# Packed attention with an MLP behind it, on one core: the held PSUM pair in a pool of its own, and another order of the inserted blocks

## The chip, the core and the metric

The kernel runs on one core of one Trainium2 chip. The metric is the device time of one execution in microseconds (us). Three runs of the kernel before gave 245.87, 245.77 and 245.65, a median of 245.77. One more execution was taken with the hardware profiler; it is the one that the rows of this document come from, and it took 245.88, of which 244.1 is the span that the profile covers. Its granted TensorE clock was 0.998 of full speed.

## What is computed

```python
def sm_attn(qq, kk, vv):
    s = scale * np.matmul(qq, kk.transpose(0, 1, 3, 2))
    a = np.exp(s - np.max(s, axis=-1, keepdims=True))
    a = a / (np.sum(a, axis=-1, keepdims=True) + 1e-09)
    return np.matmul(a, vv)
p_packed = sm_attn(p, k, v)            # 32 packed queries per head
out = sm_attn(q, p_packed, p_packed)   # 576 queries against 32 keys
x = out.transpose(0, 2, 1, 3).reshape(4608, 512)
h = x @ w_in                           # 512 x 2048
return (h * cos(h)) @ w_out            # 2048 x 512
```

There are 8 batches, 8 heads, 576 positions and a head dimension of 64.

## The kernel before

Everything but the softmax sums is done in bf16 with sums in fp32. The kernel never forms the second attention's output: for each batch it multiplies the packed result with `w_in` first (`ppw`, four pieces of 512 columns, into `PPW`), and then the normalised second softmax `a2n` with `PPW`. That gives `h` transposed, in 16 blocks of 128 of the 2048 columns (a block is called fc, 0 to 15).

The order of the work is written out by hand; tiles get their semaphores from the framework, and each engine works through its own queue in the order in which the instructions were recorded. For a batch b the steps are:

- `pe_T` (transposes of k or q on TensorE, L121) or `xbar` (by a DMA, L107), `s1` (scores and exp of the first softmax), `a1_pe`/`a1_xbar`, `pp` (packed result, L191), `pp_T` (L203), `ppw` (L218), `s2` (scores and exp of the second softmax, L148), `sums2` (L244) and `normalise`, which gives `a2n`.
- 16 blocks. `h_mm` (L268) does four matmuls of 288 columns into a pair of PSUM banks, ScalarE takes the cosine (L272), VectorE the product into `gT` (L275). Batch 0 is different: `h_one` (L294) does two matmuls of 512 columns into one bank, cosine at L299, product at L300; its last 64 rows of all blocks follow later in `h_rest` (L308), whose product goes to `joint` (L314).
- The second product of the MLP, `gT` with `w_out`, in chunks of 128 rows and 16 matmuls each. These matmuls are called fills: a generator yields them one by one, and `fill(n)` puts the next n into TensorE's queue, wherever the hand-written order has room. `out_gen` (L359) serves batches 1 to 7, `out_first` (L375) batch 0.

PSUM has 8 banks. Pool `O` holds two for the whole kernel (`ot`). The other six change owner: `banks("pairs")` makes them three pairs, A0, A1 and A2 (pool `psA`), and `banks("single")` six single banks (pool `psH`); the old pool is closed first, so the new one's tiles wait for the readers of the old. `psa` hands the pairs out in turn, as `pairs` lists them. Batch 0's 16 blocks run in the single banks, taken in rotation; behind them come the first fills of batch 0 and `ppw(1, 0)` and `ppw(1, 1)`, also in single banks, and then the pairs are opened again.

`out_first` opens four chunks of batch 0 at once: chunks 0 and 1 in the two banks of `O`, chunks 2 and 3 in a held pair, A2 (`psa(at=2)`, so it needs the pairs). It yields 4 fills of each chunk, again 4 of each, then finishes chunks 2 and 3 in the slot of batch 1, frees A2 and finishes chunks 0 and 1. `store` copies a finished chunk to `osb` with one engine (`osb_eng`, ScalarE in a slot) and issues its DMAs on SP.

```python
    set_filler(0)
    fill(4)
    for n in range(2):
        ppw(1, n, (ACT, V), own=one)
    fill(4)
    ACT.preload_act_table_set(EXP_SET)
    banks("pairs")
    fill(4)
...
    fill(4)
    s2(1)
```

Between the last two `fill(4)` stand the 24 transposes of q of batch 1 and the copies to `qT` by VectorE and ScalarE.

Batch 1's 16 `h_mm` blocks are called its slot. `slot(1, hooks, trail, heavy, weight)` puts `weight[fc]` fills behind block fc (the weights sum to 36, as many as the fills left with the 8 of batch 1 that trail) and the hooks named for that fc; `heavy[fc] = (_, n)` keeps up to n of the block's fills behind the hook. A block without an entry in `heavy` has its fills behind the hook. The hooks are `pw2` (`ppw(1, 2)` and `ppw(1, 3)`, each a pair, the first half copied by ScalarE and the second by VectorE), `h_rest(0)`, two DMA transposes on SP (k of batch 3, q of batch 2), `pack_p` (transposes of p for batches 2 and 3) and the transposes of k of batch 2 (`tk2` and `pe_T`). Behind the slot come ScalarE's table load, four fills and `s1(2)`.

Of the kernel before, what the change touches and what calls it, by code (L numbers as in the profile page):

```python
# [8 lines left out]
FP32 = mybir.dt.float32  # L9
# [6 lines left out]
def kernel(  # L16
# [19 lines left out]
    PSUM = bass.MemoryType.PSUM  # L36
# [11 lines left out]
    o_pool = ctx.enter_context(tc.tile_pool(name="o", bufs=4))  # L48
    small = ctx.enter_context(tc.tile_pool(name="small", bufs=3))
    O = ctx.enter_context(tc.tile_pool(name="psO", bufs=2, space=PSUM))  # L50
    ctx.enter_context(tc.manual_schedule())
    psum = {"stack": ctx.enter_context(ExitStack())}

    pairs, turn = [], [0]

    def banks(kind):

        psum["stack"].close()
        name, n = ("psA", 1) if kind == "pairs" else ("psH", 6)
        psum[name] = psum["stack"].enter_context(tc.tile_pool(name=name, bufs=n, space=PSUM))  # L60
        pairs[:], turn[0] = [0, 1, 2], 0

    banks("pairs")
    V, ACT, G = nc.vector, nc.scalar, nc.gpsimd

# [18 lines left out]
    def copy(eng, out, in_):  # L84
        if eng is ACT:
            ACT.copy(out=out, in_=in_)  # L86
        else:
            eng.tensor_copy(out=out, in_=in_)  # L88

    def psa(dt=FP32, at=None):  # L90

        if at is None:
            at = pairs[turn[0] % len(pairs)]
            turn[0] += 1
        return psum["psA"].tile([128, 2, 512 if dt == FP32 else 1024], dt, name="psA", tag=f"A{at}")

    def load(n, b):
        bf[n, b] = bf_pool.tile([TP, H, C * D], BF16, name=n + "bf", tag=n + "bf", bufs=1 if n == "q" else 2)
# [13 lines left out]
    def pe_T(n, b, engs=(V, V, V), groups=(0, 1, 2), own=None):  # L112
        if 0 in groups:
            xT[n, b] = att_pool.tile([128, H * 3, TP], BF16, name=n + "T", tag=n + "T", bufs=2 if n == "k" else 1)
        t = xT[n, b]
        flat = bf[n, b].rearrange("p h x -> p (h x)")
        for i in groups:
            ps = own(BF16) if own else psa(BF16)[:, 0, :]
            for j in range(8):
                o = 8 * i + j  # L120
                nc.tensor.transpose(ps[:, j * TP:(j + 1) * TP], flat[:, o * 128:(o + 1) * 128],  # L121
                                    ident[0:TP, 0:TP])
            to = t[:, 8 * i:8 * i + 8].rearrange("p a x -> p (a x)"), ps[:, 0:8 * TP]
            if engs[i] is None:
                return to
            copy(engs[i], *to)

    def bank(dt=FP32):
        return O.tile([128, 512 if dt == FP32 else 1024], dt, name="ot", tag="ot")

    def pack_p(b0, b1, flat=None):
        ng = 2 * (b1 - b0)
        if flat is None:
            flat = psa(BF16).rearrange("p a x -> p (a x)")
        for g in range(ng):
            nc.tensor.transpose(flat[:, g * 128:(g + 1) * 128],
                                p_bf[:, 2 * b0 + g].rearrange("p t d -> p (t d)"), ident)
        V.tensor_copy(out=P2[:, b0:b1].rearrange("p b h n -> p (b h n)"), in_=flat[:, 0:ng * 128])
# [67 lines left out]
    def ppw(b, n, eng=None, own=None, later=False, cuts=((0, 512),)):  # L206
        if b not in PPW:
            PPW[b] = ppw_pool.tile([128, 2, DF], BF16, name="PPW", tag="PPW")
        two = isinstance(eng, tuple)
        if own:  # L210
            ps = [own(), own()]
        else:
            t = psa()
            ps = [t[:, 0, :], t[:, 1, :]]
        for x in range(4):
            for y in range(2):
                r = slice(64 * y, 64 * y + 64)
                nc.tensor.matmul(ps[y][32 * x:32 * x + 32, :], ppT[b % 2][r, 0, x, :],  # L218
                                 w_in_bf[r, x, n * 512:(n + 1) * 512], start=True, stop=True)

        def evacuate(cuts=cuts):
            if own or two:
                for a, z in cuts:
                    for y in range(2):
                        copy(eng[y] if two else eng, PPW[b][:, y, n * 512 + a:n * 512 + z], ps[y][:, a:z])
            else:
                copy(eng or (V, ACT)[n % 2], PPW[b][:, :, n * 512:(n + 1) * 512], t)
        if later:
            return [lambda c=c: evacuate((c,)) for c in cuts]
        evacuate()  # L230

    def s2(b):
        a2u[b] = att_pool.tile([128, 2, S], BF16, name="a2u", tag="a2u")
        ps = scores(lambda r, h, e: ppT[b % 2][r, (h + e) % 2, h // 2, :], xT["q", b])
        for y in range(2):
            ACT.activation(out=a2u[b][:, y].rearrange("p (e x) -> p e x", e=2),  # L236
                           in_=ps[y][:, :, 0:HS], func=AF.Exp, scale=rs1[b][:, y:y + 1])
# [80 lines left out]
    osb_eng = [V]  # L318

    def pieces_of(b, c):  # L320
        ob = out[b * S:(b + 1) * S, :].rearrange("(p c) d -> c p d", c=C)
        if c == 4:
            o0 = out[(b - 1) * S:b * S, :].rearrange("(p c) d -> c p d", c=C)
            return [(0, 64, o0[5, 32:96]), (64, 128, ob[5, 32:96])]
        res, z = [], c * 128
        while z < c * 128 + 128:
            j, p0 = z // TP, z % TP
            n = min(TP - p0, c * 128 + 128 - z)
            res.append((z - c * 128, z - c * 128 + n, ob[2 * (j % 3) + j // 3, p0:p0 + n]))
            z += n  # L330
        return res

    def n_chunks(b):
        return 5 if b % 2 and b < B - 1 else 4

    def tail_chunk(b, c):
        osb = o_pool.tile([128, DM], FP32, name="osb")
        for i, (a, z) in enumerate(((0, 256), (256, 384), (384, 512))):
            cols = slice(a, z)
            ps = O.tile([128, z - a], FP32, name="ot", tag="ot")  # L340
            for fc in range(NFC):
# [3 lines left out]
            for (a, z, rows), q in zip(pieces_of(b, c), (nc.sync, nc.scalar)):  # L345
                q.dma_start(out=rows[:, cols], in_=osb[a:z, cols])

    def store(b, c, ps):
        osb = o_pool.tile([128, DM], FP32, name="osb")
        copy(osb_eng[0], osb, ps)  # L350
        for a, z, rows in pieces_of(b, c):
            nc.sync.dma_start(out=rows, in_=osb[a:z, :])

    def out_gen(b):
        for c in range(n_chunks(b)):
            ps = O.tile([128, DM], FP32, name="ot", tag="ot")
            for fc in range(NFC):
# [6 lines left out]
    def out_first():  # L364

        pss = {}
        for c, fcs in ((0, 4), (1, 4), (2, 4), (3, 4), (0, 8), (1, 8), (2, 8), (3, 8),
                       (2, 12), (3, 12), (2, 16), (3, 16), (0, 16), (1, 16)):
            if c not in pss:
                if c == 2:  # L370
                    held = psa(at=2)
                    pairs[:] = [0, 1]
                pss[c] = O.tile([128, DM], FP32, name="ot", tag="ot") if c < 2 else held[:, c - 2, :]
            for fc in range(8 if (c, fcs) in ((0, 16), (1, 16)) else fcs - 4, fcs):
                nc.tensor.matmul(pss[c], gT[0][:, fc, c * 128:(c + 1) * 128], w_out_bf[:, fc, :],  # L375
                                 start=(fc == 0), stop=(fc == NFC - 1))
                if fc == NFC - 1 and c == 3:
                    store(0, 2, pss[2])
                    store(0, 3, pss[3])
                    pairs[:], turn[0] = [0, 1, 2], 0  # L380
                elif fc == NFC - 1 and c < 2:
                    store(0, c, pss[c])
                yield
# [3 lines left out]
    def set_filler(b):  # L387
        filler.append([out_gen(b) if b else out_first(), 16 * n_chunks(b)])
# [4 lines left out]
    def fill(n):  # L393
        while n > 0 and filler:
            next(filler[0][0])
            filler[0][1] -= 1
            if filler[0][1] == 0:
                filler.pop(0)
            n -= 1
# [9 lines left out]
    def dup_p(a, b, eng):  # L409
        for t in range(2):  # L410
            eng.tensor_copy(out=p_bf[:, a:b, t, :], in_=p_raw[:, a:b, :])
# [74 lines left out]
    c14()()  # L486
    c15()()
    set_filler(0)
    fill(4)
    for n in range(2):  # L490
        ppw(1, n, (ACT, V), own=one)
    fill(4)
    ACT.preload_act_table_set(EXP_SET)
    banks("pairs")
    fill(4)
    t = psa(BF16)
    for i in range(2):
        pe_T("q", 1, (None,) * 3, (i,), own=lambda dt: t[:, i, :])
# [3 lines left out]
    load("q", 2)  # L502
    load("v", 2)
    dup_p(4, 2 * B, G)
    fill(4)
    s2(1)
    fill(4)
    sums2(1, 0)
# [28 lines left out]
    def pw2(b, n, eng=None):  # L537
        ppw(b, n, eng)
        ppw(b, n + 1, eng)
# [20 lines left out]
    def cross(n, b):  # L560
        return lambda: xbar(n, b)

    osb_eng[0] = ACT
    slot(1, [(5, lambda: pw2(1, 2, (ACT, V))), (6, lambda: h_rest(0)), (7, cross("k", 3)),
             (8, lambda: pack_p(2, 4)), (9, cross("q", 2)), (10, tk2), (11, lambda: pe_T("k", 2, (V, V, ACT), (2,)))],
         trail=8, heavy={5: (0, 2), 6: (0, 2)}, weight=[3, 3, 3, 3, 2, 3, 3, 2, 2, 2, 2, 2, 2, 2, 1, 1])
    ACT.preload_act_table_set(EXP_SET)
    osb_eng[0] = V
    behind(xT["q", 2][0:1, 0, 0:1])
# [110 lines left out]
```

## Time and profile before

| | |
|---|---|
| median of three runs | 245.77 us |
| the profiled execution | 245.88 us, span 244.1 us |
| TensorE matmuls | 230.0 us busy, 2208 rows |
| VectorE | 161.3 us busy, 256 rows |
| ScalarE | 167.1 us busy, 267 rows |
| batch 0's blocks, first to last product | 23.36 to 34.73 us |
| `s2(1)`, first matmul | 38.84 us |
| batch 1's slot, first matmul | 44.15 us |
| `s1(2)`, first matmul | 65.26 us |

PE is TensorE, PEld its weight loads, DVE VectorE, ACT ScalarE, POOL GpSimd, SP the engine that issues most DMAs. A row of the timeline gives start, duration, engine, line, operation, output and input tiles, and how many instructions of the kind were joined (x4). In brackets stands how long the engine was idle before and what ended that. Consecutive matmuls overlap: a matmul of 512 columns has a row of 0.38 us, but the next one starts 0.22 later, so four of them have a joint row of 1.04. A few matmul records are missing from the trace.

### The profile page before, as it was taken

Reading aid. Unit: us, or ns where it says so; the run is one execution under the profiler, and the core shown is the slowest. Engines: PE = TensorE matmul, PEld = TensorE weight load, DVE = VectorE, ACT = ScalarE, POOL = GpSimd, SP = SyncE. Lnnn points to the kernel's source line nnn. Section 1 sums busy time; section 2 is a strip of 40 time slices with the busy share of each in tenths; the row PEclk is TensorE's granted clock in tenths of the full one; section 3 lists DMA queues with packets and bytes.
Section 4 is the critical chain, followed back from the end, with each engine's and each line's share of the span. In section 5 each row is a group of like instructions: output and inputs, shape, how many; then the busy total and the mean of one; then the engine's idle time right before and its main releaser. Section 6 shows DMA issues by size and latency. Waiting matters only on the chain.

```text
span 244.1 us, 5438 instructions
## 1 busy us (share of the span) xinstructions
PE 230.0 (94%) x2208; PEld 128.1 (52%) x2244; DVE 161.3 (66%) x256; ACT 167.1 (68%) x267; POOL 37.6 (15%) x60
## 2 busy tenths in 40 slices
PE   7889889999999999999999999999999999999994
PEld 3454335556555564565546564556456554565453
DVE  3359981668658986687757787678758688787001
ACT  2349996687839868876978677876788583776110
POOL 8522212201130014005100501030100110010000
PEclk9999999999999999999999999999999999999999
DMA  6999999999799999999999995989376101311133
GB/s 94 202 205 207 205 205 227 198 228 207 143 148 195 223 202 139 219 220 189 220 182 193 156 209 107 183 168 208 69 150 142 46 0 46 86 43 46 44 85 86
DMA packets 64376, 37.37 MB, mean 153 GB/s; under 512 B 36864, under 2 KB 59776, under 8 KB 64352
## 3 DMA queue, kind: packets, MB, share of 16 engines
q0 software_dynamic: 23152, 18.75, 50.5%
q1 hardware_dynamic: 40960, 18.16, 34.7%
q8 instruction: 17, 0.28, 0.4%
q10 hardware_dynamic: 240, 0.13, 0.2%
q14 instruction: 7, 0.06, 0.1%
HBM read 37.22 MB, written 9.44 MB: 191 GB/s over the span
## 4 chain that ended last, share of the span: by engine, by line
PE 79%; DVE 7%; ACT 2%; issue 2%; ACTq 0%
PE ot L359 43%; PE psA L268 22%; DVE gT L300 3%; PE psA L375 3%; PE psA L218 2%; PE psA L148 2%; PE ot L375 1%; PE ot L342 1%; PE psA L244 1%; DVE PPW L88 1%; DVE gT L275 1%; PE psA L191 1%; ACT cosT L272 1%; PE psA L121 1%; DVE joint L314 1%
## 5 line engine op out<-in xcount | busy, mean ns | idle before, releaser
L359 PE MATMUL ot<-w_out_bf,gT 128*128 128x512 bf16 x424 | 109.8, 379 | 2.1 <-issue 1.6
L275 DVE TENSOR_TENSOR gT<-psA,cosT 128x576 bf16<-128x576 f32 x112 | 83.2, 757 | 21.9 <-ACT cosT L272 20.9
L272 ACT ACTIVATE cosT<-psA 128x576 bf16<-128x576 f32 x112 | 72.8, 654 | 25.2 <-PE psA L268 24.0
L268 PE MATMUL psA<-a2n,PPW 128*128 128x288 bf16 x448 | 73.2, 286 | 0.4
L359 PEld LDWEIGHTS <-gT 128*128 128x128 bf16 x448 | 42.2, 98 | 37.4 <-issue 4.2
L268 PEld LDWEIGHTS <-PPW 128*128 128x128 bf16 x448 | 43.7, 98 | 30.2 <-issue 0.9
L88 DVE CAST PPW<-psA 128x1024 bf16<-128x1024 f32 (+1 forms) x21 | 24.3, 1170 | 7.9 <-PE psA L218 7.9
L279 POOL COPY joint<-gT 128x512 bf16<-128x512 bf16 x14 | 8.7, 618 | 91.5 <-DVE gT L275 91.5
L88 DVE COPY osb<-ot 128x512 f32<-128x512 f32 (+2 forms) x17 | 11.0, 647 | 15.6 <-PE ot L342 14.6
L86 ACT COPY osb<-ot 128x512 f32<-128x512 f32 (+1 forms) x19 | 10.8, 568 | 14.3 <-PE ot L359 9.1
L254 DVE SCALAR_TENSOR_TENSOR a2n<-a2u,r,lns 128x576 bf16<-128x576 bf16 x16 | 12.4, 814 | 12.3 <-ACT lns L252 12.3
L246 ACT ACTIVATE lns<-psA 128x576 f32<-128x576 f32 x16 | 10.4, 652 | 7.3 <-PE psA L244 6.8
L157 ACT ACTIVATE a<-psA 128x576 bf16<-128x576 f32 x16 | 10.3, 647 | 7.3 <-PE psA L148 7.2
L359 PE MATMUL ot<-w_out_bf,joint 128*128 128x512 bf16 x45 | 14.0, 379 | 0.3 <-issue 0.2
L236 ACT ACTIVATE a2u<-psA,rs 128x576 bf16<-128x576 f32 x16 | 11.0, 738 | 1.4 <-PE psA L148 1.4
L103 POOL COPY gate<-kT 1x1 bf16<-1x1 bf16 x4 | 0.7, 181 | 64.7 <-DMA kT<-kbf 64.7
L300 DVE TENSOR_TENSOR gT<-psH,cosT 128x512 bf16<-128x512 f32 x16 | 9.9, 685 | 0.4 <-ACT cosT L299 0.4
L252 ACT ACTIVATE lns<-lns 128x576 f32<-128x576 f32 x16 | 10.0, 676 | 0.0
L218 PE MATMUL psA<-w_in_bf,ppT 64*32 64x512 bf16 x208 | 9.2, 380 | 0.4 <-DVE gT L275 0.4
L299 ACT ACTIVATE cosT<-psH 128x512 bf16<-128x512 f32 x16 | 8.9, 633 | 0.7 <-DVE gT L300 0.4
L416 PE MATMUL ot<-wz 128*128 128x512 f32 (+2 forms) x11 | 7.5, 769 | 1.9 <-DVE wz L429 1.7
L375 PE MATMUL ot<-w_out_bf,gT 128*128 128x512 bf16 x30 | 8.8, 380 | 0.1
(89 smaller groups left out, 191.9 us busy)
## 6 DMA issues: line engine op xcount, KB each, us to landing
kbf<-in_k_dram POOLq DMA_DIRECT2D x8, 576.0 KB, 13.0
vbf<-in_v_dram POOLq DMA_DIRECT2D x8, 576.0 KB, 7.9
qbf<-in_q_dram POOLq DMA_DIRECT2D x8, 576.0 KB, 10.5
out_dram<-osb SPq DMA_DIRECT2D x24, 192.0 KB, 3.9
out_dram<-osb SPq DMA_DIRECT2D x22, 128.0 KB, 2.5
w_in_bf<-in_moe_w_in_dram POOLq DMA_DIRECT2D x4, 512.0 KB, 16.9
w_out_bf<-in_moe_w_out_dram POOLq DMA_DIRECT2D x4, 512.0 KB, 21.2
out_dram<-osb SPq DMA_DIRECT2D x25, 64.0 KB, 2.7
```

The costliest lines, as they stand in the source:

```text
L86: ACT.copy(out=out, in_=in_)
L88: eng.tensor_copy(out=out, in_=in_)
L218: nc.tensor.matmul(ps[y][32 * x:32 * x + 32, :], ppT[b % 2][r, 0, x, :], w_in_bf[r, x, n * 512:(n + 1) * 512], start=True, stop=True)
L236: ACT.activation(out=a2u[b][:, y].rearrange("p (e x) -> p e x", e=2), in_=ps[y][:, :, 0:HS], func=AF.Exp, scale=rs1[b][:, y:y + 1])
L246: ACT.activation(out=lns[b][:, y].rearrange("p (e x) -> p e x", e=2), in_=ps[:, :, 0:HS], func=AF.Ln)
L254: V.scalar_tensor_tensor(out=a2n[b][:, y], in0=a2u[b][:, y], scalar=r1[b][:, y:y + 1], in1=lns[b][:, y], op0=ALU.mult, op1=ALU.mult)
L268: nc.tensor.matmul(ps[:, e, 0:HS], PPW[b][:, y, fc * 128:(fc + 1) * 128], a2n[b][:, y, e * HS:(e + 1) * HS], start=(y == 0), stop=(y == 1))
L272: ACT.activation(out=csv, in_=ps[:, :, 0:HS], func=AF.Sin, bias=PI_HALF)
L275: V.tensor_tensor(out=gT[b][:, fc, :].rearrange("p (e x) -> p e x", e=2), in0=ps[:, :, 0:HS], in1=csv, op=ALU.mult)
L300: return lambda: V.tensor_tensor(out=gT[b][:, fc, 0:512], in0=ps, in1=cs, op=ALU.mult)
L359: nc.tensor.matmul(ps, w, w_out_bf[:, fc, :], start=(fc == 0), stop=(fc == NFC - 1))
L375: nc.tensor.matmul(pss[c], gT[0][:, fc, c * 128:(c + 1) * 128], w_out_bf[:, fc, :], start=(fc == 0), stop=(fc == NFC - 1))
```

## The change

The pair A2 gets a pool of its own, `psX`, which stays open for the whole kernel; `psH` and the pool of pairs share the remaining four banks. So `banks("single")` gives four banks, and the held pair can be used while the single banks are still open. In the order before `s2(1)`, chunks 0 and 1 get their first 4 fills each ahead of `ppw(1, 0)`, chunks 2 and 3 theirs ahead of the change of banks, and none stand between the transposes of q and `s2(1)`. Chunk 2 of batch 0 is copied by VectorE. In the slot, three hooks come one or more blocks later, and the weights and the places of the fills at fc 5 and 6 change; the sum of the weights is 36 as before.

```diff
+    X = ctx.enter_context(tc.tile_pool(name="psX", bufs=1, space=PSUM))
...
-        name, n = ("psA", 1) if kind == "pairs" else ("psH", 6)
+        name, n = ("psA", 1) if kind == "pairs" else ("psH", 4)
...
-        return psum["psA"].tile([128, 2, 512 if dt == FP32 else 1024], dt, name="psA", tag=f"A{at}")
+        pool = X if at == 2 else psum["psA"]
+        return pool.tile([128, 2, 512 if dt == FP32 else 1024], dt, name="psA", tag=f"A{at}")
...
-    def store(b, c, ps):
+    def store(b, c, ps, eng=None):
         osb = o_pool.tile([128, DM], FP32, name="osb")
-        copy(osb_eng[0], osb, ps)
+        copy(eng or osb_eng[0], osb, ps)
...
-                    store(0, 2, pss[2])
+                    store(0, 2, pss[2], V)
                     store(0, 3, pss[3])
...
     set_filler(0)
-    fill(4)
+    fill(8)
     for n in range(2):
         ppw(1, n, (ACT, V), own=one)
-    fill(4)
     ACT.preload_act_table_set(EXP_SET)
+    fill(8)
     banks("pairs")
-    fill(4)
+    pairs[:] = [0, 1]
     t = psa(BF16)
...
-    fill(4)
     s2(1)
...
     slot(1, [(5, lambda: pw2(1, 2, (ACT, V))), (6, lambda: h_rest(0)), (7, cross("k", 3)),
-             (8, lambda: pack_p(2, 4)), (9, cross("q", 2)), (10, tk2), (11, lambda: pe_T("k", 2, (V, V, ACT), (2,)))],
-         trail=8, heavy={5: (0, 2), 6: (0, 2)}, weight=[3, 3, 3, 3, 2, 3, 3, 2, 2, 2, 2, 2, 2, 2, 1, 1])
+             (9, lambda: pack_p(2, 4)), (9, cross("q", 2)), (11, tk2), (12, lambda: pe_T("k", 2, (V, V, ACT), (2,)))],
+         trail=8, heavy={5: (0, 1), 6: (0, 4)}, weight=[3, 3, 3, 3, 2, 4, 5, 2, 1, 2, 2, 2, 1, 1, 1, 1])
```

## The prediction

> **What bounds the kernel now.** I read the page's busy shares and its chain first, then the timeline of the two stretches that the diff touches: 28 to 39 us (end of batch 0's blocks to `s2(1)`) and 48 to 66 us (batch 1's slot).
>
> ```profile
> PE 230.0 (94%) x2208; PEld 128.1 (52%) x2244; DVE 161.3 (66%) x256; ACT 167.1 (68%) x267; POOL 37.6 (15%) x60
> ...
> PE 79%; DVE 7%; ACT 2%; issue 2%; ACTq 0%
> ```
>
> TensorE is busy for 94% of the span and carries 79% of the chain that ended last. So the time changes by what is added to or taken from TensorE's holes; the other engines matter where TensorE waits for them. The change removes no instruction: it moves matmuls, moves one copy from ScalarE to VectorE, and takes two buffers from batch 0's loop. The granted clock is 0.998, so no row is stretched.
>
> The first stretch, in order of time (start, duration, engine, line; in brackets the idle time before and what ended it):
>
> ```profile
> 28.58 2.19 PE L294 MATMUL psH<-a2n,PPW 128*128 128x512 bf16 x9 [0.16 <-issue]
> ...
> 30.43 4.30 DVE L300 TENSOR_TENSOR gT<-psH,cosT 128x512 bf16<-128x512 f32 x7 [0.40 <-ACT cosT L299]
> ...
> 30.70 0.56 PE L191 MATMUL ot<-vbf,a1T 96*32 96x64 bf16 x48
> ...
> 32.08 0.35 PE L203 MATMUL ot<-ident,pp_sb 128*128 128x128 bf16 x2
> ...
> 34.04 1.04 PE L375 MATMUL ot<-w_out_bf,gT 128*128 128x512 bf16 x4
> ...
> 35.99 1.04 PE L375 MATMUL psA<-w_out_bf,gT 128*128 128x512 bf16 x4 [0.91 <-DVE PPW L88]
> ...
> 36.86 1.19 PE L121 MATMUL psA<-ident,qbf 96*128 96x96 bf16 x24
> 37.80 0.96 DVE L499 COPY qT<-psA 128x1536 bf16<-128x1536 bf16 x1 [1.87 <-PE psA L121]
> ...
> 38.84 0.56 PE L148 MATMUL psA<-qT,ppT 64*32 64x288 bf16 x16
> ```
>
> Here VectorE sets the pace of the blocks (seven products in a row from 30.43), while TensorE runs ahead of it: block 13's two matmuls are the last of the nine at 28.58, at 30.18 and 30.39. The hole before 35.99 is the pool change: the held pair lies in banks that `PPW`'s copies still read. The four fills after the transposes (from 37.88) cover the `qT` copy that `s2(1)` waits for at 38.84.
>
> The second stretch:
>
> ```profile
> 48.90 1.08 ACT L86 COPY osb<-psA 128x512 f32<-128x512 f32 x2
> 48.93 0.76 DVE L275 TENSOR_TENSOR gT<-psA,cosT 128x576 bf16<-128x576 f32 x1 [0.38 <-ACT cosT L272]
> ...
> 49.85 1.22 ACT L272 ACTIVATE cosT<-psA 128x576 bf16<-128x576 f32 x2
> ...
> 50.56 1.42 DVE L275 TENSOR_TENSOR gT<-psA,cosT 128x576 bf16<-128x576 f32 x2 [0.87 <-ACT cosT L272]
> ...
> 51.37 0.41 PE L218 MATMUL psA<-w_in_bf,ppT 64*32 64x512 bf16 x8 [0.42 <-DVE gT L275]
> ...
> 52.16 0.65 PE L268 MATMUL psA<-a2n,PPW 128*128 128x288 bf16 x4
> ...
> 65.26 0.44 PE L148 MATMUL psA<-kT,P 64*32 64x288 bf16 x16
> ```
>
> After the two `osb` copies the cosines of blocks 4 and 5 are late, then their products on VectorE, then the matmuls at 51.37 and 52.16 that need the pairs of those products.
>
> **Part 1: four single banks instead of six.** Block fc takes the buffer that block fc-4 leaves (fc-6 before). Laid along TensorE's queue, blocks 5 to 12 lose nothing: they wait at most 0.1 us, and their cosines come later than that on ScalarE anyway. Block 13 needs block 9's product, the first of the seven: 30.43 + 0.69 (its row, alone) = 31.12, and 0.06 for the release (VectorE's copy ends at 24.64, the matmul behind it starts at 24.70), so 31.18 instead of 30.18: **+1.00**. Queued behind it on TensorE stand `pp(1)`, blocks 14 and 15 and `pp_T(1)`; `pp_T(1)` goes from 32.08 to 33.08. ScalarE waits for these: `pp_sb` 32.30, cosine 13 until 33.26, `ppT` 33.46 to 33.91, cosines 14 and 15 until 34.40 and 34.90. VectorE's last product ends at 35.72 instead of 34.73.
>
> **Part 2: order of the fills before `s2(1)`.** The hole in front of the held pair goes, since the pair's pool is never closed. TensorE was free at 34.92 (last of the fills at 34.04 starts at 34.70, 0.22 each) and went on at 35.99: **-1.07**. What is late next: the second `ppw(1)` block needs the buffer of block 15, whose product now ends at 35.72. TensorE arrives, after eight fills (33.52 to 35.28) and the first block, at 35.58, and gets it at 35.78: **+0.20**. And `s2(1)` now stands straight behind the transposes. It needs the `qT` copy, whose pace is fixed: `s2(1)` comes 1.98 after the first transpose (36.86 to 38.84). The four fills that covered this were moved ahead, so their 4 x 0.217 = **0.87** is open again. Sum of both parts: 1.00 - 1.07 + 0.20 + 0.87 = +1.00; followed row by row, transposes at 37.87 and `s2(1)` at 39.85 against 38.84. From there to the slot's first matmuls (44.15) both TensorE and the softmax chain start at `s2(1)`, so +1.00 stays.
>
> Bounds: without any wait of block 13, 0.00 for this pair of parts; with the full 0.96 between the last transpose and `s2(1)` open and 0.4 at `ppw`, +1.3. I take 1.0, because every term comes from a row beside it.
>
> **Part 3: chunk 2's copy on VectorE.** I expect it to be worse, not better. Both copies read one held pair, and in the built program ScalarE's copy of chunk 3 no longer waits for TensorE but for VectorE: for VectorE's copy of chunk 2. On before's clock (the 1.0 left out): VectorE finishes block 3's product at 49.69 and copies until 50.30 (0.69, as the `osb` copy at 66.70). ScalarE's copy then runs 50.35 to 50.94, and cosine 4 starts at 50.85 instead of 49.85. Behind ScalarE's waiting copy stand cosines 4 and 5; product 4 comes at 51.55 (50.56), product 5 ends at 52.98 (51.98). Block 6's matmuls need the latter's pair: 53.03 instead of 52.16. Ahead of it TensorE did one fill more, worth 0.22, so it has lost 0.65.
>
> No row of before shows two engines in the halves of one pair at once: for `PPW` the second half starts on VectorE at 52.50, after ScalarE's end at 52.44, for `kT` at 60.12 after 60.08, but VectorE was busy until then both times. The Trainium skill, "PSUM — Partial Sum Buffer", Specifications (TRN2), says that ScalarE and VectorE read PSUM in parallel as long as they are in different banks, which these two copies are. By that rule this part would help rather than hurt, which is the second rival below.
>
> **Part 4: weights and hooks of the slot.** I go on in the same way: each start is the later of TensorE's own queue and the release of its pair plus 0.06, with durations from the rows of these blocks (four matmuls 0.49, a fill 0.22, `h_rest` 0.9, cosine 0.65, product 0.76, `cosR` 1.02, `joint` 1.22). `h_rest` starts at 53.72 behind the second half of `PPW` on VectorE (53.57); cosR runs from 54.87, `joint` ends at 57.14; block 9 now takes that pair and starts at 57.20, `pack_p` behind product 7 at 57.86, block 10 at 58.74. By fc 9 there are 28 fills done instead of 26, two more in front of the waits of fc 5 to 9: block 10's 58.74 stands against 57.91 with two fills (0.43) more done, a loss of 0.40. The transposes of `k` (24 x 0.042) now fall to fc 11 and 12, and fc 13 to 15 carry one fill each: 0.49 + 0.22 = 0.71 per block is less than VectorE's 0.76, and ScalarE has the third `kT` copy (0.82) among the cosines. TensorE waits there for products, most before block 14, which needs product 12 (62.65 to 63.41) and so starts at 63.47, 0.35 after the queue was free. Five fills follow block 15 (64.17). `s1(2)` comes at 65.83 instead of 65.26: parts 3 and 4 together **+0.57**. Bounds: -0.5 if the copies don't wait for each other, +1.0 if all of cosine 4's delay arrives at the end.
>
> **Queues.** SP issues the stores of chunks 2 and 3 about 0.9 later within the slot; behind them stand the two DMA transposes (56.44 for 3.49, 60.12 for 3.08), the stores of chunks 0 and 1, and on POOL the next loads (gate at 66.52). Shifted by 1.9 the second ends at 65.1; its reader `s2(2)` comes at 72.44 and the gate at 66.52, both shifted by 1.6 too. I cost this at nothing; without that cover it is the 0.9.
>
> **Sum.** From 65 us on the order is the same and TensorE-bound, so nothing is won back. Profiled execution 245.88 + 1.00 + 0.57 = 247.45; it lies 0.11 above the median of 245.77, so against the median **247.3 us**.
>
> **The rivals.**
> - *The waits are shorter than laid out.* VectorE's or TensorE's next rows close up and half of the terms arrive: 246.3 to 246.6. For it: four buffers times 0.62 per product exceed one block's way through the three engines (0.43 + 0.6 + 0.69). Against: at block 13 TensorE is a whole us ahead of VectorE. Chance 0.16.
> - *The two copies run side by side.* Then ScalarE's ends at 49.49, cosine 4 comes 0.45 earlier than before, and `s1(2)` by 0.5: 245.77 + 1.0 - 0.5 = 246.3. This is the rule of the Trainium skill named above. Against: the program's own wait. Chance 0.06.
> - *Faster.* The hole of 1.07 goes and nothing takes its place: this needs block 13 not to wait (TensorE at block 13 later than block 9's product, 31.12, which the row at 28.58 speaks against) and something else in front of `s2(1)`. By 0.4 to 1.0: 244.8 to 245.3. It decides at block 13: each 0.1 us that it starts before 31.18 is won. Chance 0.05.
> - *Nothing measurable.* 245.3 to 246.2 (within 0.2%, 0.49 us, about what a measurement of this kernel tells from no change): parts 1 and 2 cancel and the slot costs under 0.5. Chance 0.09.
> - *The forecast*, 246.7 to 247.9: chance 0.64.
>
> The range goes from 246.2 (the first two rivals) to 248.0 (both upper bounds taken by half). Slower by over 0.2%: 0.64 + 0.16 + 0.06 = 0.86; within: 0.09; faster: 0.05.
>
> **What would show it.** Right: matmuls of block 13 (L296) idle until VectorE's gT product; no idle before the psA fills; a hole of 0.8 to 0.9 between transposes and `s2(1)`, released by VectorE's `qT` copy; ScalarE idle before `osb<-psA` until VectorE's `osb`. Wrong: TensorE at `pp(1)` still near 30.7, `s2(1)` before 39.3, or ScalarE's `osb` copy at once behind cosine 3.

## The result, and the profile after

The changed kernel takes **247.12 us** (median of four runs, 247.09 to 247.23); the kernel before took 245.76 (245.65 to 245.87) beside it. The ratio is 1.0056, with a 95% interval of 1.0039 to 1.0074: slower by 1.36 us. The profiled execution took 247.23, of which the span is 245.4 (244.1 before), at a granted clock of 1.0.

The page after, busy shares and the chain that ended last:

```profile
PE 231.3 (94%) x2209; PEld 128.5 (52%) x2244; DVE 162.3 (66%) x257; ACT 166.8 (68%) x266; POOL 37.4 (15%) x60
...
PE 81%; DVE 5%; issue 2%; ACT 2%; DVEq 0%; ACTq 0%
```

The page shows nearly nothing: the same share of TensorE, a chain with 2% more TensorE in it. (Its 1.3 us more of busy time are no new work: a matmul row ends by a model, and a joint row counts a wait between two of its matmuls as busy.) The difference has to be read in the two stretches. The timeline after, 29 to 40 us (start, duration, engine, line, operation; in brackets the idle time before it and its releaser):

```profile
30.55 2.48 DVE L302 TENSOR_TENSOR gT<-psH,cosT 128x512 bf16<-128x512 f32 x4 [0.40 <-ACT cosT L301]
...
31.29 0.59 PE L296 MATMUL psH<-a2n,PPW 128*128 128x512 bf16 x2 [0.49 <-DVE gT L302]
31.82 0.55 PE L193 MATMUL ot<-vbf,a1T 96*32 96x64 bf16 x48
...
33.18 0.28 PE L205 MATMUL ot<-ident,pp_sb 128*128 128x128 bf16 x2
33.29 1.89 PE L377 MATMUL ot<-w_out_bf,gT 128*128 128x512 bf16 x8
...
33.49 0.37 ACT L87 COPY ppT<-ot 128x256 bf16<-128x256 bf16 x1 [0.16 <-PE ot L205]
...
34.39 1.29 DVE L302 TENSOR_TENSOR gT<-psH,cosT 128x512 bf16<-128x512 f32 x2 [0.34 <-ACT cosT L301]
35.11 1.03 PE L220 MATMUL psH<-w_in_bf,ppT 64*32 64x512 bf16 x16
...
36.07 1.90 PE L377 MATMUL psA<-w_out_bf,gT 128*128 128x512 bf16 x8
...
37.81 1.19 PE L123 MATMUL psA<-ident,qbf 96*128 96x96 bf16 x24
38.75 0.96 DVE L501 COPY qT<-psA 128x1536 bf16<-128x1536 bf16 x1 [1.83 <-PE psA L123]
...
39.76 0.59 PE L150 MATMUL psA<-qT,ppT 64*32 64x288 bf16 x16 [0.76 <-DVE qT L501]
```

The seven products in a row of before are four now (30.55), and block 13's matmuls stand at 31.29 behind a wait for VectorE. The eight fills of the held pair (36.07) carry no bracket: that hole is gone. A new one of 0.76 stands in front of `s2(1)` at 39.76, released by VectorE's `qT` copy. The timeline after, 48 to 54 us, and the row that ends the slot:

```profile
50.55 0.68 DVE L89 COPY osb<-psA 128x512 f32<-128x512 f32 x1
...
51.27 0.58 ACT L87 COPY osb<-psA 128x512 f32<-128x512 f32 x1 [1.42 <-DVE osb L89]
51.75 1.20 ACT L274 ACTIVATE cosT<-psA 128x576 bf16<-128x576 f32 x2
...
52.44 1.42 DVE L277 TENSOR_TENSOR gT<-psA,cosT 128x576 bf16<-128x576 f32 x2 [1.20 <-ACT cosT L274]
...
53.25 0.41 PE L220 MATMUL psA<-w_in_bf,ppT 64*32 64x512 bf16 x8 [0.93 <-DVE gT L277]
...
66.59 0.44 PE L150 MATMUL psA<-kT,P 64*32 64x288 bf16 x16
```

ScalarE is idle for 1.42 until VectorE has copied chunk 2. Then it copies chunk 3 and does cosines 4 and 5 back to back; the wait goes on to VectorE's products and to TensorE at 53.25.

For the runs below a few starts are enough. The first product of batch 0 comes at 23.20 to 23.77 in the profiles, though the instructions up to there are the same in all kernels (those with six single banks lie at 23.20 to 23.61, those with four at 23.23 to 23.77), so the starts are taken from it. "To `s2(1)`" is from the first product to the first matmul of `s2(1)`, "slot" from the slot's first matmul to that of `s1(2)`.

| kernel | to `pp(1)` | end of last product | to `s2(1)` | slot |
|---|---|---|---|---|
| before | 7.34 | 11.37 | 15.48 | 21.11 |
| after | 8.33 | 12.19 | 16.27 | 21.50 |

So the first stretch lost 16.27 - 15.48 = 0.79 and the slot 0.39. From `s2(1)` to the slot it is 5.31 before and 5.33 after, from `s1(2)` to the end 178.84 and 178.83. Batch 0's products started 0.13 later in the profile of after (23.49 and 23.36). The sum, 0.79 + 0.39 + 0.02 - 0.01 + 0.13 = 1.32, is the difference of the spans (245.4 and 244.1).

Each kernel has one profile, but several share the order of a stretch and repeat each other: "to `s2(1)`" is 15.46 to 15.48 in the five profiles with before's first stretch and 16.27 in all three with after's. So differences of 0.1 in these columns mean something, where the 95% intervals of the times are 0.1 to 0.2% (0.2 to 0.5 us) to either side.

### The profile page after: what moved, and what is told of

Read it like the earlier page. It is cut to its first block, busy times and chain, and to the rows that moved or that the text cites. A ratio compares the mean times of both kernels' runs of the same rounds, so it can differ in the third digit from the quotient of the medians.

```text
span 245.4 us, 5440 instructions
## 1 busy us (share of the span) xinstructions
PE 231.3 (94%) x2209; PEld 128.5 (52%) x2244; DVE 162.3 (66%) x257; ACT 166.8 (68%) x266; POOL 37.4 (15%) x60
## 4 chain that ended last, share of the span: by engine, by line
PE 81%; DVE 5%; issue 2%; ACT 2%; DVEq 0%; ACTq 0%
PE ot L361 42%; PE psA L270 22%; PE psA L377 3%; PE ot L377 3%; PE psA L220 2%; PE psA L150 2%; DVE gT L302 2%; DVE gT L277 2%; PE ot L344 1%; PE psA L246 1%; PE psA L193 1%; ACT cosT L274 1%; DVE PPW L89 1%; PE psH L296 1%; PE psA L123 1%
## 5 line engine op out<-in xcount | busy, mean ns | idle before, releaser
L361 PE MATMUL ot<-w_out_bf,gT 128*128 128x512 bf16 x424 | 110.0, 379 | 2.2 <-issue 1.7
L296 PE MATMUL psH<-a2n,PPW 128*128 128x512 bf16 x30 | 8.9, 380 | 1.1 <-DVE gT L302 0.5
```

The costliest lines, as they stand in the source:

```text
L296: nc.tensor.matmul(ps, PPW[b][:, y, fc * 128:(fc + 1) * 128], a2n[b][:, y, 0:512], start=(y == 0), stop=(y == 1))
L361: nc.tensor.matmul(ps, w, w_out_bf[:, fc, :], start=(fc == 0), stop=(fc == NFC - 1))
```

## The experiments

My theory after the result: four terms, each from one part of the change, that add up. The rival was that a part costs only together with another.

### The first stretch: banks, the pool of its own, the fills

`e9_four_buffers`, the kernel before with fewer single banks alone:

```diff
-        name, n = ("psA", 1) if kind == "pairs" else ("psH", 6)
+        name, n = ("psA", 1) if kind == "pairs" else ("psH", 4)
```

> The kernel before with one figure changed: its pool of single banks holds four instead of six; the held pair's pool is still opened behind the last products, and the order of the slot is as before. Theory: the number of banks alone makes block 13 of batch 0 late, so that the batched PP starts about 8.3 us behind the first product of batch 0 instead of 7.34, and the last product ends some 0.8 later than before; the idle stretch ahead of the held pair stays, since its pool still waits for the last reader; the slot keeps its length of 21.1. That gives 246.4 to 246.9. Rival: four banks cost only together with the moved fills, the gap ahead of the batched PP stays under 0.3 us and the time is 245.8 to 246.1.

`e5_pool_alone`, the same and the held pair in its own pool; order of the fills, copies and slot as before:

```diff
+    X = ctx.enter_context(tc.tile_pool(name="psX", bufs=1, space=PSUM))
...
-        name, n = ("psA", 1) if kind == "pairs" else ("psH", 6)
+        name, n = ("psA", 1) if kind == "pairs" else ("psH", 4)
...
+        pool = X if at == 2 else psum["psA"]
...
+    pairs[:] = [0, 1]
```

> The kernel before with the pool of its own for the held pair and four single banks, and nothing else: order of the fills, copies and slot as before. Theory: block 13 waits as in the changed kernel, the hole in front of the held pair goes, the four fills behind the transposes stay, but the second ppw(1) block now waits for the last product with only four fills in front of it; s2(1) comes 0.6 to 0.9 us later than before, the slot is unchanged: 246.5 to 246.8 us. Rival (without the moved fills the pool is a gain, by the hole of 1.07 us): 244.9 to 245.6 us.

`e3_fills_behind`, the kernel after with four fills back in front of `s2(1)`:

```diff
-    fill(8)
+    fill(4)
     banks("pairs")
...
+    fill(4)
     s2(1)
```

> The changed kernel with four of the eight fills in front of the change of banks put behind the transposes of q, where four stood before. Theory: they cover the wait of s2(1) for the copy of qT; the transposes come 0.87 us earlier and s2(1) with them: 246.2 to 246.4 us. Rival (s2(1) waits for another thing than that copy, or ScalarE's table load ends last): 246.9 to 247.2 us.

`e4_block13_x`, the kernel after with block 13 in the first bank of the held pair, which is still empty then:

```diff
-    c13 = h_one(0, 13)
+    x13 = psa(at=2)
+    c13 = h_one(0, 13, own=lambda: x13[:, 0, :])
```

> The changed kernel with block 13 of batch 0 in the first bank of the held pair, which is free then; so it has five buffers at the point in question. Theory (block 13 waits for block 9's product because of four buffers, and the three steps behind it wait with it): block 13 starts 1.0 us earlier, the last product of batch 0 about 0.9 us earlier, s2(1) 0.8 to 0.95 us earlier: 246.2 to 246.4 us. Rival (the delay at block 13 is absorbed, and the second ppw(1) block's wait comes from VectorE's pace): 246.8 to 247.2 us.

| kernel | us | before on that chip | ratio, 95% | to `pp(1)` | last product | to `s2(1)` |
|---|---|---|---|---|---|---|
| e9_four_buffers | 246.78 | 245.83 | 1.0036, 1.0023 to 1.0048 | 8.32 | 12.19 | 16.30 |
| e5_pool_alone | 246.40 | 246.00 | 1.0016, 0.9999 to 1.0033 | 8.32 | 12.19 | 15.94 |
| e3_fills_behind | 246.50 | 245.93 | 1.0014, 0.9998 to 1.0029 | 8.33 | 12.19 | 15.55 |
| e4_block13_x | 246.55 | 245.93 | 1.0023, 1.0014 to 1.0032 | 7.67 | 11.53 | 15.61 |

The number of banks alone makes block 13 late; no fill has to be moved for it. The timeline of e9, the lines of its own:

```profile
31.03 0.59 PE L294 MATMUL psH<-a2n,PPW 128*128 128x512 bf16 x2 [0.50 <-DVE gT L300]
...
36.67 1.04 PE L375 MATMUL psA<-w_out_bf,gT 128*128 128x512 bf16 x4 [0.18 <-DVE PPW L88]
```

The second line is the hole in front of the held pair. It was 0.91 idle before and was expected to stay; in e9 it is 0.18, because TensorE itself arrives later there. So the pool of its own has little left to win once the banks are four: 16.30 - 15.94 = 0.36 in e5, whose rows at the same place are

```profile
34.30 1.29 DVE L302 TENSOR_TENSOR gT<-psH,cosT 128x512 bf16<-128x512 f32 x2 [0.34 <-ACT cosT L301]
...
35.04 0.65 PE L220 MATMUL psH<-w_in_bf,ppT 64*32 64x512 bf16 x8 [0.48 <-DVE gT L302]
...
36.50 1.03 PE L377 MATMUL psA<-w_out_bf,gT 128*128 128x512 bf16 x4
```

with no hole at the held pair, and 0.48 of waiting at the second `ppw(1)` block for VectorE. It is not the last product that this block waits for, as was expected, but the one before: the block starts at 35.04, when the first of the two products of the row at 34.30 has just ended (34.30 + 0.69 = 34.99). In e3 eight fills stand ahead of these blocks and four in front of `s2(1)`. The idle 0.48 is gone, though not all of the waiting (the joint row of the 16 `ppw` matmuls takes 1.03 in e3, as in after), and `s2(1)` is covered again. Its timeline:

```profile
36.14 1.04 PE L377 MATMUL psA<-w_out_bf,gT 128*128 128x512 bf16 x4
37.13 1.18 PE L123 MATMUL psA<-ident,qbf 96*128 96x96 bf16 x24
...
38.15 1.03 PE L377 MATMUL psA<-w_out_bf,gT 128*128 128x512 bf16 x4
39.10 0.56 PE L150 MATMUL psA<-qT,ppT 64*32 64x288 bf16 x16
```

No bracket stands at `s2(1)`. Step by step from before to after: 15.48 + 0.82 (four banks, e9) - 0.36 (own pool, e5) - 0.39 (eight fills ahead of `ppw`, e3) + 0.72 (four fills taken from in front of `s2(1)`, after) = 16.27.

e4 gives block 13 a bank that nobody holds. In its timeline the bracket at block 13 is gone:

```profile
30.67 2.48 DVE L302 TENSOR_TENSOR gT<-psH,cosT 128x512 bf16<-128x512 f32 x4 [0.40 <-ACT cosT L301]
30.76 0.59 PE L296 MATMUL psA<-a2n,PPW 128*128 128x512 bf16 x2
31.28 0.56 PE L193 MATMUL ot<-vbf,a1T 96*32 96x64 bf16 x48
```

But `pp(1)` comes only 8.33 - 7.67 = 0.66 earlier, not the 0.99 that four banks cost. The other 0.33 is the waiting of the blocks ahead of block 13, which e4 leaves in four banks. The times of e3 and e4 lie 0.1 and 0.15 above what was expected, e5 0.1 below. The intervals of e5 and e3 just include 1, so the sizes of these steps rest on the starts in the profiles and not on the times.

### Chunk 2's copy

`e6_vector_alone`, the kernel before with the copy of chunk 2 on VectorE and nothing else:

```diff
...
-                    store(0, 2, pss[2])
+                    store(0, 2, pss[2], V)
```

> The kernel before with chunk 2's copy on VectorE, and nothing else. Theory: cosine 4 starts 1.0 us later, the slot gets 0.5 to 0.9 us longer: 246.4 to 246.8 us. Rival (it costs only with the changed kernel's weights, which put more fills behind blocks 5 and 6): 245.8 to 246.1 us.

`e1_both_scalar`, the kernel after with that copy back on ScalarE:

```diff
-                    store(0, 2, pss[2], V)
+                    store(0, 2, pss[2])
```

> The changed kernel with chunk 2's copy back on ScalarE; everything else as changed. Theory (ScalarE's copy of chunk 3 waits for VectorE's copy of chunk 2, and cosines 4 and 5 stand behind it): ScalarE copies both from about the end of cosine 3 without waiting, cosine 4 starts 0.8 to 1.0 us earlier relative to block 3, the slot gets 0.4 to 0.7 us shorter: 246.4 to 246.7 us. Rival (the engine of that copy does not matter, the slot's cost is that of the weights and hooks): 247.0 to 247.2 us.

`e2_chunk3_first`, the kernel after with the two stores exchanged, so that VectorE's copy waits for ScalarE's instead:

```diff
-                    store(0, 2, pss[2], V)
                     store(0, 3, pss[3])
+                    store(0, 2, pss[2], V)
```

> The changed kernel with the two store lines exchanged: ScalarE copies chunk 3 first, VectorE then copies chunk 2. Each engine still copies one chunk, but now VectorE waits for ScalarE and not the other way. Theory: cosine 4 comes 1.3 to 1.5 us earlier relative to block 3 than in the changed kernel, and the slot gets 0.8 to 1.1 us shorter: 246.0 to 246.3 us. Rival (a copy on VectorE in itself delays the products behind it): no better than with both copies on ScalarE, 246.5 us or more.

| kernel | us | before on that chip | ratio, 95% | cosine 4 from the slot's start | slot |
|---|---|---|---|---|---|
| before | | | | 5.70 | 21.11 |
| after | | | | 6.66 | 21.50 |
| e6_vector_alone | 246.91 | 246.00 | 1.0031, 1.0015 to 1.0048 | 6.66 | 22.04 |
| e1_both_scalar | 246.40 | 245.93 | 1.0018, 0.9999 to 1.0037 | 5.70 | 20.63 |
| e2_chunk3_first | 246.27 | 245.93 | 1.0025, 1.0009 to 1.0042 | 5.24 | 20.64 |

The copy costs 22.04 - 21.11 = 0.93 alone and 21.50 - 20.63 = 0.87 in the changed kernel. In the timeline of e2 ScalarE does not wait:

```profile
49.10 0.65 ACT L274 ACTIVATE cosT<-psA 128x576 bf16<-128x576 f32 x1 [0.49 <-PE psA L270]
49.75 0.59 ACT L87 COPY osb<-psA 128x512 f32<-128x512 f32 x1
50.24 0.65 ACT L274 ACTIVATE cosT<-psA 128x576 bf16<-128x576 f32 x1
50.46 0.68 DVE L89 COPY osb<-psA 128x512 f32<-128x512 f32 x1
```

Same two engines, same two copies, and 0.86 of the slot comes back: it was the order of the two, not VectorE's work, that cost. That cosine 4 then comes 0.46 earlier than in e1 wins nothing more; at 5.70 it is no longer what the slot waits for. e6 came out 0.1 above its expectation, and e1's slot shrank by 0.87 where 0.4 to 0.7 was expected.

### The weights and the places in the slot

`e7_slot_alone`, the kernel before with the new places and the new weights (the last two lines of the change's diff):

> The kernel before with the changed kernel's hooks and weights of batch 1's slot, and nothing else. Theory (the slot's loss is all that of the copy, and hooks and weights gain): the slot gets 0.4 to 0.5 us shorter: 245.4 to 245.6 us. Rival, part 4 of the prediction (the one-fill blocks at the end leave TensorE waiting, hooks and weights gain nothing): 245.9 to 246.2 us.

`e10_hooks_alone`, the kernel before with the new places (three hooks, each one block later), old weights:

```diff
-             (8, lambda: pack_p(2, 4)), (9, cross("q", 2)), (10, tk2), (11, lambda: pe_T("k", 2, (V, V, ACT), (2,)))],
+             (9, lambda: pack_p(2, 4)), (9, cross("q", 2)), (11, tk2), (12, lambda: pe_T("k", 2, (V, V, ACT), (2,)))],
```

> The kernel before with the new places of the inserted steps in batch 1's slot (9, 9, 11, 12) and the old weights. Theory: the places carry the gain of 0.47 us that the slot showed with places and weights together, because the packing of P then no longer waits 0.53 us for VectorE's joint rows: the slot is 20.6 to 20.7 us long instead of 21.1, and the time is 245.4 to 245.6. Rival: the weights carry it, the slot stays at 21.0 to 21.2, and the time is 245.8 to 246.1.

`e11_weights_alone`, the kernel before with the new weights, old places:

```diff
-         trail=8, heavy={5: (0, 2), 6: (0, 2)}, weight=[3, 3, 3, 3, 2, 3, 3, 2, 2, 2, 2, 2, 2, 2, 1, 1])
+         trail=8, heavy={5: (0, 1), 6: (0, 4)}, weight=[3, 3, 3, 3, 2, 4, 5, 2, 1, 2, 2, 2, 1, 1, 1, 1])
```

> The kernel before with the new weights of the slot's blocks (which say how many fills stand behind each) and the old places of the inserted steps. Theory: without the new places the weights gain nothing, the slot is 21.0 to 21.3 us long and the time is 245.8 to 246.2. Rival: the weights carry the gain, the slot is 20.6 to 20.7 us long and the time is 245.4 to 245.6.

| kernel | us | before on that chip | ratio, 95% | slot |
|---|---|---|---|---|
| e7_slot_alone | 245.52 | 246.00 | 0.9979, 0.9963 to 0.9996 | 20.64 |
| e10_hooks_alone | 245.51 | 245.83 | 0.9989, 0.9980 to 0.9997 | 20.78 |
| e11_weights_alone | 245.32 | 245.83 | 0.9982, 0.9973 to 0.9991 | 20.63 |

Part 4 is a gain of 0.47 by itself. The view of the waits of TensorE in the slot (what waited, for whom: us in total, times, longest) says of before

```profile
PE psA L136 <- DVE joint L314: 0.5, 1, 0.5
PE psA L218 <- DVE gT L275: 0.4, 1, 0.4
```

of e10

```profile
PE psA L218 <- DVE gT L275: 0.4, 1, 0.4
```

and of e11

```profile
PE psA L268 <- DVE gT L275: 0.5, 2, 0.3
```

while e7's has no row. The places take away the wait of `pack_p` for the `joint` rows, and 0.33 is won. The weights put three fills instead of one in front of `ppw(1, 2)`, cover the wait of 0.42 behind it and that of `pack_p`, and 0.48 is won, though two small waits of the blocks come in their place. My theory that the places carry the gain fell: the weights alone give all of it. The two together, with no row left in that view, are still no shorter than the weights alone (20.64 and 20.63). The view leaves out short waits, and e7 has some. In its timeline block 14 starts at 62.58, behind one fill from 62.09. The next matmul can start 0.22 behind a fill, so 0.27 is a wait; it ends 0.05 after VectorE's product that began at 61.77 and took 0.76. How much of the missing gain such waits make up stays open.

The slot's two terms nearly add: 0.93 - 0.47 = 0.46, against 0.39 for both in after. Behind the late cosine the weights and places win 22.04 - 21.50 = 0.54. In the first stretch the parts do not add: what one is worth depends on the others that are there.

### Putting it together

`e8_five_buffers`, the kernel after with the exchange of e2, the four fills of e3, and blocks 8 and 13 both in the first bank of the held pair, so that batch 0's blocks have a fifth buffer:

```diff
-        h_one(0, fc)()()
+        x8 = psa(at=2) if fc == 8 else None
+        h_one(0, fc, own=(lambda: x8[:, 0, :]) if fc == 8 else None)()()
...
-    c13 = h_one(0, 13)
+    x13 = psa(at=2)
+    c13 = h_one(0, 13, own=lambda: x13[:, 0, :])
```

> The changed kernel with chunk 3 stored first, four fills behind the transposes of q, and blocks 8 and 13 of batch 0 in the first bank of the held pair, so that from block 8 on there are five buffers in rotation. Theory: no wait of TensorE at blocks 9 to 13, last product of batch 0 as early as before, no hole before the held pair, s2(1) 0.8 to 0.95 us earlier than before, slot 0.48 us shorter: 244.4 to 244.8 us, faster than both kernels. Rival (the gains overlap, since each alone brought the kernel back to the time before and something else then ends last): 245.4 to 245.9 us.

It takes 245.22 against 246.00 (ratio 0.9963, 0.9946 to 0.9981): faster than both kernels, but between the 244.4 to 244.8 expected and the rival's 245.4 to 245.9. `pp(1)` is back at 7.33 and the slot is 20.64, so both costs of the change are gone. The saving in front of `s2(1)` did not come in the profiled execution: 15.41, against 15.48 before. The timeline of e8 shows where it went:

```profile
33.43 1.90 PE L377 MATMUL ot<-w_out_bf,gT 128*128 128x512 bf16 x8 [0.56 <-DMA w_out_bf<-in_moe_w_out_dram]
...
37.20 1.18 PE L123 MATMUL psA<-ident,qbf 96*128 96x96 bf16 x24 [0.35 <-DVE PPW L89]
```

The first fills now stand ready before their weights have landed, and the transposes of q wait 0.35 for a bank that VectorE's `PPW` copy still reads. In this execution the two stretches win 0.07 + 0.47 = 0.54. But the profile fell on one of the two longest of e8's twelve executions (245.72; five took 244.93 to 245.03), and by the medians the gain is 0.78. The wait for the weights may belong to this execution in part: the first fill, released by their landing, comes 33.43 - 23.77 = 9.66 behind the first product here and 32.52 - 23.36 = 9.16 in before. What the shorter executions waited for is not shown. By their ratios e8, e7 and e11 can't be told apart.

## Why the prediction was right

The forecast was 247.3 (246.7 to 247.9 as a case); 247.12 was measured. The costs came where they were laid and by the waits that were named, with two exceptions: a third of block 13's lateness has another source, and the weights and places, costed at next to nothing, are a gain. The sum of each stretch was some 0.2 too large, and the split into terms was less right than the sums.

- **Block 13 (+1.00).** `pp(1)` came 8.33 - 7.34 = 0.99 later, behind the wait for VectorE that was named. But 0.33 of it is the waiting of the blocks ahead of block 13 (e4), of which the prediction said that they lose nothing or 0.1 each. The end was right since block 13 waits for block 9's product whether or not TensorE was slowed before.
- **VectorE's last product (+0.99).** It was 12.19 - 11.37 = 0.82. ScalarE's part of the chain was laid out too long: the copy of `ppT` starts at 33.49, which is 33.36 on before's clock (0.13 taken off), for 33.46, and takes 0.37 for 0.45. So the last product ends at 34.39 + 1.29 - 0.13 = 35.55 for 35.72. This 0.17 is most of the 0.21 by which the sum of the stretch was too large.
- **The second `ppw(1)` block (+0.20).** The chain was laid out with the gap of 0.44 between `pp_T(1)` and the first fill in before (32.08, 32.52). In before that gap held a wait of 0.22 for the DMA of `w_out` (its row is shown at the end); in after the data had landed, and the gap is 0.11 (33.18, 33.29). The fills start 0.36 earlier than laid out on before's clock, so the block waits longer than the 0.20 said: the joint row takes 1.03, against 0.62 in e8, so about 0.41. TensorE waits there for the same product either way, so this does not move `s2(1)`.
- **The hole (-1.07) and the open `qT` copy (+0.87).** Both are seen, the second as 0.76 idle where 0.8 to 0.9 had been named. Their sizes hold only in the order in which they were priced. With four banks the hole shrinks by itself, so the own pool wins 0.36 (e5 against e9), and putting the fills behind the transposes again wins 0.72 (e3). Parts 1 and 2 together: +0.79 for +1.00.
- **Chunk 2's copy.** Cosine 4 came 6.66 - 5.70 = 0.96 later for 1.00 predicted, by the named wait: ScalarE idle for 1.42 until VectorE's `osb`. At the end of the slot 0.87 of it is left (e1), 0.93 without the other parts (e6). The forecast's end of VectorE's copy, 50.30, does not follow from 49.69 and a row of 0.69. It fits all the same, since the copy starts 0.09 before the row of block 3's product ends (50.55; 49.88 + 0.76) and so ends at 50.55 + 0.68 - 0.94 = 50.29 on before's slot clock.
- **Weights and places.** Here the prediction went wrong in its reason. It worked them out on top of the late cosine and let 0.65 of loss at block 6 become 0.40 at block 10 and 0.57 at the end, so it gave them next to nothing. They win 0.47 by themselves (e7), in before's two waits of 0.53 and 0.42, and 0.54 behind the late cosine (e6 and after). The second stood in the prediction's own lines (51.37), but neither was counted as something that could be won. Block 10 was laid at 58.74; it came at 59.52, which is 58.58 on before's slot clock (59.52 - 45.09 + 44.15), and the 0.16 stays to the end. The wait laid before block 14 is there: 0.27 in e7 and after (63.74 to 64.23, less a fill's 0.22), for 0.35. Parts 3 and 4 together: +0.39 for +0.57.
- **Queues.** Nothing was lost behind the slot: from `s1(2)` to the end 178.83 us, for 178.84 before.

The rival of shorter waits (246.3 to 246.6) is out, and that of two copies side by side too: ScalarE's copy starts when VectorE's has ended. Whether the two engines could read the halves of one pair at once no run here shows. The Trainium skill, "PSUM — Partial Sum Buffer", Specifications (TRN2), says that they access PSUM in parallel as long as there is no bank collision. For single banks the trace of after agrees: ScalarE's two `PPW` copies run from 35.58 for 1.20 and VectorE's from 35.62 for 1.30. For a pair, in after and e6 the program's wait puts the copies one behind the other, and in e2 VectorE's copy starts at 50.46 after ScalarE's has ended at 50.34. The rival's price, 0.5 off the slot, is about what e2 shows (0.47), but not for its reason: e1, with cosine 4 no earlier than before, has the same slot, so the weights and places win it and the earlier cosine nothing.

The range held the time, though its upper end has a slip: half of both upper bounds gives 247.3 + 0.15 + 0.22 = 247.7, and 248.0 is about both in full. That the number came so near is in part luck. From the first product on the kernel lost 1.19 us where 1.57 was laid out; 0.13 more in the spans is the later start of batch 0's products in that profile, which is no part of the change.

## What to carry to other kernels

In this kernel a buffer taken from a rotating pool was paid where the producer ran furthest ahead of the slowest reader. Look there first, and give that one block a buffer that is empty anyway: that brought 0.66 of the 0.99 back (e4). Moving work into a hole can open the hole that the work covered (0.76 in front of `s2(1)` here), and the prices of such moves depend on the order in which they are made. So price the whole order and check the parts one by one. When two engines copy halves of one tile, look at which one is made to wait: put first the engine that has the more urgent work behind its copy (0.86 here, e2).

## What the runs showed of the hardware

- The DMA of the first part of `w_out`, 512 KB, is issued by POOL at 11.3 us in before, 11.4 in after and 11.7 in e8; the four parts landed 21.0 to 21.7 us after their issue. The timeline of before, weight loads (PEld), shows who waited:

```profile
32.51 0.55 PEld L375 LDWEIGHTS <-gT 128*128 128x128 bf16 x4 [0.22 <-DMA w_out_bf<-in_moe_w_out_dram]
```

  So it is a floor for the first fill at about 32.5 to 33.4, which before just touches (0.22), after doesn't (33.29, no wait), and e8 runs into (0.56). Here a load of the beginning bounded a place 21 us after its issue.
- The first product of batch 0 came between 23.20 and 23.77 us in the profiles of kernels whose instructions don't differ up to there. That spread of 0.57 is of the size of the effects here, so starts were compared from that point on, and times as medians of 4 to 12 runs.
